# One load behind a transpose, one pair of norms ahead of a statistic: an order of work by hand in an MLP mixer kernel

## The chip, the cores and the metric

The kernel runs on one core of a Trainium2 chip. The core has five engines with instruction streams of their own: TensorE (PE; its weight loads are shown as PEld), VectorE (DVE), ScalarE (ACT), GpSimd (POOL) and SyncE (SP), which here only issues DMAs. They meet at semaphores. The metric is the device time of one execution in microseconds, as the median of several runs.

## The reference

The input x has 2048 tokens of 512 numbers in bf16; w1 and w2 are 512 by 512, w3 is 512 by 1792, w4 is 1792 by 512.

```
h  = gelu(layernorm(x) @ w1)
g0, g1, g2, g3 = the four quarters of h's 512 columns, shifted along
                 the tokens by +1, -1, +2, -2, zeros at the edge
x1 = x + concat(g0, g1, g2, g3) @ w2
out = x1 + gelu(layernorm(x1) @ w3) @ w4
```

The layer norms subtract the mean and divide by the square root of the variance plus 1e-5; they have no weights.

## The kernel before

The 2048 tokens are 16 tiles of 128. Tile t holds tokens t, t + 16, t + 32 and so on, one per partition, so that a shift by one or two tokens reads a neighbouring tile, and only the edges wrap. All weights and all tiles stay in SBUF. The eight PSUM banks are handed out by hand.

The first layer (norm, w1, gelu) is made in two ways.

Tiles 0 to 5 go raw: x is transposed as it is (tiles 0 to 3 by TensorE and ACT, `tp0` to `tp3` and `ev0` to `ev3`; tiles 4 and 5 by one transposing DMA straight from DRAM, `tdx_4`), multiplied by w1 (`m1r`, L378), copied to SBUF (`rc`, L388) and normed afterwards: `zr` (L393, DVE) takes off mean times column sum of w1, `g1r` (L399, ACT) scales and applies gelu, and a transposing DMA `th` (L357) puts the result in place. Their statistics are needed late.

Tiles 6 to 15 go in pairs and are normed first. For each tile DVE makes statistics `st0_t` (L289, bn_stats), and from them an aggregate `ag0_t` (L294); for each pair GpSimd raises the variances to the power of minus one half, `rs0_t` (L300); DVE applies both, `nm0_t` (L309). Pairs 8 and 10 are transposed by TensorE (`tp8`, `tp10`, L323) and evacuated by ACT (`ev8`, `ev10`, L332); pairs 6, 12 and 14 by a transposing DMA issued on SP, `td0_t` (L343). Then come a matmul with w1 per pair (`m1p`, L410) and gelu into a transposed buffer (`g1p` L420, or `g1s` L425 tile by tile).

The second product is `m2_t`, four matmuls per tile, one per shifted quarter; for tiles 8 to 15 it is cut into parts (L450), each of which waits for its own neighbours, and for tiles 0 to 7 not (L436). Tiles 14 and 15 need tiles 0 and 1 in their last parts, by the wrap of the tokens, and so wait for `th_0`. `x1_t` (L460, DVE) adds x. The second norm works as the first, with `td1` transposes. Tiles 8 to 15 come first in the second layer, then 0 to 7: `m3h_0_0_0` (L492), the first product with w3, takes tiles 8 and 9 and waits for `td1_8`. Then follow the products with w3 by blocks of four tiles (L468) and with w4 (L511), the last sum (L523) and the stores (L527).

The order on each engine is written out by hand: `firsts` (L637 to L652) names the operations of each engine in order, and what is not named follows as it was added. Nothing reorders them later; an engine that waits holds up all that stands behind it. Semaphore waits are derived from what each operation reads and writes. Nearly all DMAs are issued on SP, in the order of `firsts["sp"]`; the first loads of w1 and that of x1 on ACT's queue. A load `ldxT` may take several tiles (`load_x(t, n)`, L271): its consumers wait for the whole of it.

Around the change, SP issues the loads of x10, x11 and x12, then `td0_6`, which waits for `nm0_7`, then x13, x14 with x15, the four loads of w2, one for each 128 rows, then `td0_12` and `td0_14`. DVE meanwhile goes through statistics, aggregates and norms of tiles 6 to 15. On PE the six `m1r` are followed by `tp8`, `m1p6`, `tp10`, `m1p8`, `m1p10`.

Of the kernel before, what the change touches and what calls it, by code (L numbers as in the profile page):

```python
# [5 lines left out]
P = 128  # L6
# [20 lines left out]
class Program:  # L27
# [7 lines left out]
    def add(self, eng, name, fn, reads=(), writes=(), dma=False):  # L35
        self.ops.append(Op(name, eng, fn, reads, writes, dma))
# [135 lines left out]
def bass_standalone__mixer_s_mlp__prompt_kernel(nc: bass.Bass, x, w1, w2, w3, w4, out):  # L172
# [4 lines left out]
    DC = D // P  # L177
# [10 lines left out]
    with ExitStack() as es:  # L188
# [14 lines left out]
        w2_sb = sb("w2_sb", [P, DC, D], BF16)  # L203
# [41 lines left out]
        add = pr.add  # L245
# [25 lines left out]
        def load_x(t, n, eng="sp"):  # L271
            add(eng, f"ldx{t}", lambda e: e.dma_start(x_sb[:, t : t + n, :], xd[:, t : t + n, :]),  # L272
                writes=[(("x", i), 0) for i in range(t, t + n)], dma=True)
# [269 lines left out]
                writes=[(("w1", c), 0)], dma=True)  # L543

        def load_w2(c):
            add("sp", f"ldw2{c}", lambda e: e.dma_start(w2_sb[:, c, :], w2[P * c : P * (c + 1), :]),
                writes=[(("w2", c), 0)], dma=True)

        def load_w3a(c):
            add("sp", f"ldw3a{c}",  # L550
# [11 lines left out]
        load_w1(2, "act")  # L562
        load_w1(3, "sp")
        load_x(1, 1, "act")
        for t, n in ((6, 1), (7, 1), (2, 1), (8, 1), (3, 1), (9, 1), (10, 1), (11, 1), (12, 1), (13, 1), (14, 2), (4, 2)):
            load_x(t, n)
        for c in range(DC):
            load_w2(c)
        for c in range(DC):
            load_w3a(c)  # L570
# [56 lines left out]
        for t in (8, 10):  # L627
# [9 lines left out]
        firsts = {}  # L637
# [2 lines left out]
            m2_12b m2_13b m2_14a m2_15a m2_12 m2_13 m2_14b m2_15b m2_14 m2_15""".split()  # L640
        firsts["act"] = """ldw10 ldw12 ldx1 table ev0 ev1 rc0 ev2 ev3 rc1 rc2 rc3 rc4 rc5 ev8 cse g1p6 ev10 g1p8 g1s10 g1s11
            g1r0 g1r1 g1p12 g1p14 g2h_0_0_0 g2h_0_0_4 g1r2 g1r3 g2h_0_0_8 g2h_0_0_12 g1r4 g1r5""".split()
        firsts["dve"] = """pada padb padc padd pade padf st0_0 st0_6 st0_7 ag0_6 ag0_7
            st0_8 nm0_6 nm0_7 st0_9 ag0_8 ag0_9 st0_10 st0_11 nm0_8 nm0_9 ag0_10 ag0_11
            st0_12 nm0_10 nm0_11 st0_13 ag0_12 ag0_13 st0_14 st0_15 ag0_14 ag0_15 nm0_12 nm0_13 st0_1 ag0_0 ag0_1
            nm0_14 nm0_15 zr0 zr1 x1_8 x1_9 st1_8 st1_9 ag1_8 ag1_9 st0_2 nm1_8 nm1_9 st0_3 ag0_2 ag0_3 x1_10 x1_11 st1_10
            st1_11 ag1_10 ag1_11 x1_12 nm1_10 nm1_11 x1_13 x1_14 x1_15 zr2 zr3 st0_4 st0_5 ag0_4 ag0_5 zr4 zr5
            st1_12 st1_13 ag1_12 ag1_13""".split()
        firsts["pool"] = """ident0 ident1 neghalf stz ste rs0_6 rs0_8 rs0_10
            rs0_12 rs0_14 rs0_0 rs1_8 rs0_2 rs1_10""".split()  # L650
        firsts["sp"] = """ldx0 ldw11 ldx6 ldw13 ldx7 ldx2 ldx8 ldx3 ldx9 tdx_4 ldx10 ldx11 ldx12 td0_6 ldx13 ldx14 ldw20 ldw21 ldw22 ldw23 td0_12 td0_14 ldw3a0 ldw3a1
            ldw3a2 ldw3a3 th_0 td1_8 ldw3b ldx4 td1_10 th_2 th_4 td1_12 td1_14 ldw4""".split()  # L652

        slots = [4, 0, 2]
# [111 lines left out]
```

## Time and profile before

| what | us |
|---|---|
| median of 3 runs | 136.62 (136.54 to 136.63) |
| the profiled execution | 136.32 |
| its span, first to last instruction | 134.5 |
| PE busy | 130.8 |
| DVE busy | 58.3 |
| ACT busy | 46.8 |
| POOL busy | 12.5 |
| granted TensorE clock | 1.0 in the whole span |

Times within the profile are counted from the start of the span. A row of a timeline gives start, length, engine, line, operation, what is written and read, how many instructions in a row are merged, and in brackets the idle time of the engine before it and what ended it. SPq is the queue of SyncE: its rows are the time that it takes to issue a DMA, not the transfer. A DMA view gives the time from the issue to the landing of the last byte as the semaphore tells it. The chain of waits is followed back from the last instruction, at each step to what released it.

### The profile page before, as it was taken

How to read it: one execution, taken by the hardware profiler on the slowest of the kernel's cores; microseconds unless marked ns; L12 is line 12 of the kernel's file. 1: busy time of each engine (PE TensorE's matmuls, PEld its weight loads, DVE VectorE, ACT ScalarE, POOL GpSimd, SP SyncE). 2: the span in 40 equal slices, each digit the busy share in tenths (PEclk: the TensorE clock that was granted, in tenths of full speed). 3: DMA queues.
4: the chain of work that ended last, by engine and by line, in shares of the span. 5: the costliest groups of instructions: out<-in, count | busy, mean ns of one | idle time of the engine just before them, and what ended most of it. 6: DMA issues, size and time to landing. Idle time of an engine off the chain costs nothing.

```text
span 134.5 us, 1794 instructions
## 1 busy us (share of the span) xinstructions
PE 130.8 (97%) x719; PEld 69.6 (52%) x729; DVE 58.3 (43%) x135; ACT 46.8 (35%) x56; POOL 12.5 (9%) x25
## 2 busy tenths in 40 slices
PE   7999999999999999999999999999999999999993
PEld 2446857678884444444444444444444444444452
DVE  0689999799967777762222000122200002322222
ACT  3488871507962036550001555200066630000000
POOL 2042422220330012220000000000000000000000
PEclk9999999999999999999999999999999999999999
DMA  4999379984465984444121000011110001111121
GB/s 123 317 247 217 115 145 246 255 292 83 78 128 100 295 262 78 78 80 78 39 68 49 5 0 0 0 39 39 41 37 5 0 0 39 39 39 39 44 75 42
DMA packets 24376, 12.96 MB, mean 96 GB/s; under 512 B 16688, under 2 KB 23600, under 8 KB 24368
## 3 DMA queue, kind: packets, MB, share of 16 engines
q1 hardware_dynamic: 23792, 12.42, 36.5%
q10 hardware_dynamic: 576, 0.43, 1.0%
q8 instruction: 6, 0.10, 0.3%
q14 instruction: 2, 0.02, 0.1%
HBM read 6.82 MB, written 2.10 MB: 66 GB/s over the span
## 4 chain that ended last, share of the span: by engine, by line
PE 89%; SPq 4%; DMA 2%; DVE 2%; issue 1%
PE ps L511 36%; PE ps L468 27%; PE ps L492 9%; PE ps L410 7%; PE ps L436 5%; PE ps L450 5%; DMA x_sb<-in_x_dram 2%; SPq L272 2%; SPq L351 1%; DVE st L289 1%; PE ps L323 1%; SPq L542 1%; DVE xn L309 0%; DVE o_sb L523 0%
## 5 line engine op out<-in xcount | busy, mean ns | idle before, releaser
L511 PE MATMUL ps<-w_sb,h2T 128*128 128x512 bf16 (+2 forms) x232 | 48.1, 366 | 0.3
L523 DVE TENSOR_TENSOR o_sb<-ps,x_sb 128x512 bf16<-128x512 f32 (+2 forms) x17 | 11.2, 660 | 61.2 <-PE ps L511 61.2
L479 ACT ACTIVATE h2T<-ps 128x1024 bf16<-128x1024 f32 x21 | 21.5, 1023 | 46.2 <-PE ps L468 46.2
L468 PE MATMUL ps<-x1nT,w_sb 128*128 128x512 bf16 x168 | 36.7, 379 | 0.0
L511 PEld LDWEIGHTS ps<-w_sb,h2T 128*128 128x128 bf16 x238 | 22.8, 98 | 25.9
L468 PEld LDWEIGHTS ps<-x1nT,w_sb 128*128 128x128 bf16 x168 | 16.4, 98 | 19.8
L289 DVE BATCH_NORM_STATS2 st<-x_sb 128x6 f32<-128x512 bf16 x32 | 20.9, 682 | 4.1 <-DMA x_sb<-in_x_dram 4.0
L300 POOL TENSOR_TENSOR rstd<-mv,neghalf 128x2 f32<-128x2 f32 x16 | 11.6, 725 | 46.1 <-DVE mv L294 46.1
L492 PE MATMUL ps<-x1nT,w_sb 128*128 128x256 bf16 x112 | 12.4, 273 | 0.0
L492 PEld LDWEIGHTS ps<-x1nT,w_sb 128*128 128x128 bf16 x112 | 11.0, 98 | 1.5
L460 DVE TENSOR_TENSOR x_sb<-ps,x_sb 128x512 bf16<-128x512 f32 x16 | 10.6, 685 | 2.5 <-PE ps L436 1.5
L410 PE MATMUL ps<-xnT,w_sb 128*128 128x256 bf16 x80 | 9.2, 273 | 0.0
L503 ACT ACTIVATE h2T<-ps 128x1024 bf16<-128x1024 f32 (+1 forms) x8 | 7.1, 913 | 6.0 <-PE ps L492 6.0
L410 PEld LDWEIGHTS ps<-xnT,w_sb 128*128 128x128 bf16 x80 | 7.6, 98 | 1.2
L309 DVE TENSOR_SCALAR x1n<-x_sb,mv,rstd 128x512 bf16<-128x512 bf16 x16 | 5.9, 409 | 5.3 <-POOL rstd L300 5.3
L450 PE MATMUL ps<-w_sb,hTf 128*128 128x512 bf16 x30 | 7.0, 379 | 0.1
L436 PE MATMUL ps<-w_sb,hTf 128*128 128x512 bf16 x31 | 6.9, 379 | 0.1
L378 PE MATMUL ps<-w_sb,xnT 128*128 128x512 bf16 x23 | 6.0, 382 | 0.1
L420 ACT ACTIVATE hTf<-ps 128x1024 bf16<-128x1024 f32 x4 | 4.1, 1023 | 4.2 <-PE ps L410 4.2
L332 ACT ACTIVATE xnT<-ps 128x512 bf16<-128x512 bf16 (+1 forms) x6 | 4.4, 738 | 2.3 <-PE ps L323 2.2
L436 PEld LDWEIGHTS ps<-w_sb,hTf 128*128 128x128 bf16 x32 | 3.1, 98 | 3.6
L294 DVE BATCH_NORM_AGGREGATE mv<-st 128x2 f32<-128x9 f32 x32 | 5.0, 185 | 0.0
(28 smaller groups left out, 36.8 us busy)
## 6 DMA issues: line engine op xcount, KB each, us to landing
out_dram<-o_sb SPq DMA_DIRECT2D x15, 128.0 KB, 1.8
w_sb<-in_w_dram SPq DMA_DIRECT2D x1, 1792.0 KB, 7.7
x_sb<-in_x_dram SPq DMA_DIRECT2D x11, 128.0 KB, 3.3
w_sb<-in_w_dram SPq DMA_DIRECT2D x4, 256.0 KB, 4.2
w_sb<-in_w_dram SPq DMA_DIRECT2D x6, 128.0 KB, 3.5
w_sb<-in_w_dram SPq DMA_DIRECT2D x1, 768.0 KB, 4.8
x_sb<-in_x_dram SPq DMA_DIRECT2D x2, 256.0 KB, 4.4
w_sb<-in_w_dram ACTq DMA_DIRECT2D x2, 128.0 KB, 3.2
```

The costliest lines, as they stand in the source:

```text
L289: add("dve", f"st{layer}_{t}", lambda e: e.bn_stats(st9[:, i, 0:6], src[:, t, :]), reads=[(r, 0)], writes=[(("st6", i), 0)])
L300: lambda e: e.tensor_tensor(rstd[:, i : i + n], mv[:, i : i + n, 1], neghalf[:, 0:n], ALU.pow),
L410: ins = e.matmul(dst, w1_sb[:, c, P * fc : P * (fc + 1)], xnT[:, t : t + 2, c, :], start=(c == 0), stop=(c == DC - 1))
L436: ins = e.matmul(bank(b), hTf[:, c0 : c0 + P], w2_sb[:, j, :], start=(j == 0), stop=(j == DC - 1))
L450: ins = e.matmul(bank(b), hTf[:, w[0] : w[0] + P], w2_sb[:, j, :], start=first and n == 0, stop=last and n == len(js) - 1)
L460: lambda e: e.tensor_tensor(x1_sb[:, t, :], bank(b), x_sb[:, t, :], ALU.add),
L468: ins = e.matmul(bank(b), w3_sb[:, c, P * fc : P * (fc + 1)], x1nT[:, 4 * q : 4 * q + 4, c, :], start=(c == 0), stop=(c == DC - 1))
L479: lambda e: e.activation(h2T[:, fc : fc + 2, q % 2, :], src, ACT_F.Gelu_apprx_tanh),
L492: ins = e.matmul(dst, w3_sb[:, c, P * (fc + i) : P * (fc + i + 1)], x1nT[:, t : t + 2, c, :], start=(c == 0), stop=(c == DC - 1))
L503: lambda e: e.activation(h2T[:, fc : fc + n, q % 2, 256 * k : 256 * (k + 1)], src, ACT_F.Gelu_apprx_tanh),
L511: ins = e.matmul(ps[:, 512 * b : 512 * b + c1 - c0], h2T[:, fc, q % 2, P * i : P * (i + 1)], w4_sb[:, fc, c0:c1], start=(fc == 0), stop=(f ...
L523: lambda e: e.tensor_tensor(o_sb[:, k % 4, c0:c1], ps[:, 512 * b : 512 * b + c1 - c0], x1_sb[:, t, c0:c1], ALU.add),
```

## The change

Four edits to the order and to the loads, none to what is computed.

- DVE's order: `nm0_8` and `nm0_9` stand between `st0_10` and `st0_11` instead of after both. `ag0_6` stands before `st0_7` instead of after it. `st0_1` takes the place of `st0_12`, and `st0_12` stands with `st0_13` behind `nm0_11`.
- SP's order: the load of x12 stands behind `td0_6` instead of before it.
- x12 and x13 are one load of 256 KB instead of two of 128 KB.
- w2 comes in two loads of 256 KB instead of four of 128 KB. A part of `m2` then waits for the half in which its rows lie.

```diff
         def load_w2(c):
-            add("sp", f"ldw2{c}", lambda e: e.dma_start(w2_sb[:, c, :], w2[P * c : P * (c + 1), :]),
-                writes=[(("w2", c), 0)], dma=True)
+            add("sp", f"ldw2{c}",
+                lambda e: e.dma_start(w2_sb[:, c : c + 2, :],
+                                      w2[P * c : P * (c + 2), :].rearrange("(c p) f -> p c f", p=P)),
+                writes=[(("w2", c + i), 0) for i in range(2)], dma=True)
...
-        for t, n in ((6, 1), (7, 1), (2, 1), (8, 1), (3, 1), (9, 1), (10, 1), (11, 1), (12, 1), (13, 1), (14, 2), (4, 2)):
+        for t, n in ((6, 1), (7, 1), (2, 1), (8, 1), (3, 1), (9, 1), (10, 1), (11, 1), (12, 2), (14, 2), (4, 2)):
             load_x(t, n)
-        for c in range(DC):
+        for c in range(0, DC, 2):
             load_w2(c)
...
-        firsts["dve"] = """pada padb padc padd pade padf st0_0 st0_6 st0_7 ag0_6 ag0_7
-            st0_8 nm0_6 nm0_7 st0_9 ag0_8 ag0_9 st0_10 st0_11 nm0_8 nm0_9 ag0_10 ag0_11
-            st0_12 nm0_10 nm0_11 st0_13 ag0_12 ag0_13 st0_14 st0_15 ag0_14 ag0_15 nm0_12 nm0_13 st0_1 ag0_0 ag0_1
+        firsts["dve"] = """pada padb padc padd pade padf st0_0 st0_6 ag0_6 st0_7 ag0_7
+            st0_8 nm0_6 nm0_7 st0_9 ag0_8 ag0_9 st0_10 nm0_8 nm0_9 st0_11 ag0_10 ag0_11
+            st0_1 nm0_10 nm0_11 st0_12 st0_13 ag0_12 ag0_13 st0_14 st0_15 ag0_14 ag0_15 nm0_12 nm0_13 ag0_0 ag0_1
...
-        firsts["sp"] = """ldx0 ldw11 ldx6 ldw13 ldx7 ldx2 ldx8 ldx3 ldx9 tdx_4 ldx10 ldx11 ldx12 td0_6 ldx13 ldx14 ldw20 ldw21 ldw22 ldw23 td0_12 td0_14 ldw3a0 ldw3a1
+        firsts["sp"] = """ldx0 ldw11 ldx6 ldw13 ldx7 ldx2 ldx8 ldx3 ldx9 tdx_4 ldx10 ldx11 td0_6 ldx12 ldx14 ldw20 ldw22 td0_12 td0_14 ldw3a0 ldw3a1
```

## The prediction

> **What bounds the kernel now.** I read the page first, then the chain of waits, then the timeline of each engine around the one place where the chain leaves TensorE. The page's first part:
>
> ```profile
> PE 130.8 (97%) x719; PEld 69.6 (52%) x729; DVE 58.3 (43%) x135; ACT 46.8 (35%) x56; POOL 12.5 (9%) x25
> ```
>
> TensorE is busy nearly always, so an edit can only gain where PE has a hole, or lose by opening one. The chain that ended last, in order of time (start, length, what):
>
> ```profile
> 6.42 3.24 DMA x_sb<-in_x_dram
> ...
> 9.68 1.29 DVE st L289 x2
> 10.97 0.64 DVE xn L309 x2
> ...
> 11.66 0.62 PE ps L323 x8
> 12.28 1.81 PE ps L410 x16
> ```
>
> Before 11.66 us it runs over the load of x10, the statistics of tiles 10 and 11 and the two norms of pair 8; after 11.66 it is all PE to 132.2. The PE timeline there:
>
> ```profile
> 11.16 0.38 PE L378 MATMUL ps<-w_sb,xnT 128*128 128x512 bf16 x1
> 11.66 0.62 PE L323 MATMUL ps<-ident,xn 128*128 128x128 bf16 x8
> 12.16 1.92 PE L410 MATMUL ps<-xnT,w_sb 128*128 128x256 bf16 x16
> ```
>
> The durations include pipelining, so holes are read from starts. Matmuls of this 512-wide form start 0.216 us apart when nothing holds them (the 12 of tiles 3 to 5 start at 8.79, 9.01, 9.22 ...). The last of tile 5 started at 11.165; the next slot was 11.381, but the first transpose of pair 8 (tp8) started at 11.660. That hole is 0.279 us. The eight transposes start 0.056 apart, so the slot after them was 12.117; m1p6 started at 12.165, a hole of 0.048. Together 0.327. Behind that, PE starts follow without a hole to 28.27, and later ones are 0.05 at a time, tied to other PE work. So the most that these edits can win is about 0.33 us.
>
> What ended the two holes: VectorE and the queue of SyncE (SP).
>
> ```profile
> 5.89 0.69 DVE L289 BATCH_NORM_STATS2 st<-x_sb 128x6 f32<-128x512 bf16 x1 [0.23 <-DMA x_sb<-in_x_dram]
> 6.50 0.32 DVE L294 BATCH_NORM_AGGREGATE mv<-st 128x2 f32<-128x9 f32 x2
> ...
> 9.68 1.29 DVE L289 BATCH_NORM_STATS2 st<-x_sb 128x6 f32<-128x512 bf16 x2 [0.47 <-DMA x_sb<-in_x_dram]
> 10.88 0.72 DVE L309 TENSOR_SCALAR xn<-x_sb,mv,rstd 128x512 bf16<-128x512 bf16 x2
> ...
> 12.58 0.74 DVE L309 TENSOR_SCALAR xn<-x_sb,mv,rstd 128x512 bf16<-128x512 bf16 x2 [0.23 <-POOL rstd L300]
> ```
> ```profile
> 6.42 1.52 SPq L272 DMA_DIRECT2D x_sb<-in_x_dram  x3
> 8.41 1.24 SPq L343 DMA_TRANSPOSE xnT<-xn  x1
> 9.69 1.06 SPq L272 DMA_DIRECT2D x_sb<-in_x_dram  x2
> ...
> 16.43 2.68 SPq L343 DMA_TRANSPOSE xnT<-xn  x2
> 19.15 2.01 SPq L551 DMA_DIRECT2D w_sb<-in_w_dram  x4
> 21.20 1.61 SPq L357 DMA_TRANSPOSE hTf<-hraw  x1
> 23.65 1.32 SPq L343 DMA_TRANSPOSE x1nT<-x1n  x1
> ```
>
> nm0_9 ends at 11.602 and releases tp8. Pair 6's transpose td0_6, issued at 8.41, releases m1p6; the DMA view of that issue alone, and of the 256 KB load of x14 (issued 10.31):
>
> ```profile
> xnT<-xn SPq DMA_TRANSPOSE x1, 3.7
> ```
> ```profile
> x_sb<-in_x_dram SPq DMA_DIRECT2D x1, 256.0 KB, 3.9
> ```
>
> So td0_6 landed at 12.12, and m1p6 started 0.046 later: tp8 alone being earlier would gain nothing, since m1p6 would wait for td0_6 instead.
>
> **The change part by part.** The sum is made on the profiled execution (136.32 us: span 134.5 and 1.8 around it); the median of the runs is 136.62, 0.30 above, and I carry the difference over to it.
>
> *Pair 8's norms ahead of st0_11.* rs0_8 is done at 9.99, so nm0_8 follows st0_10 directly: DVE starts are 0.61 apart after a statistic and 0.31 after a norm, hence nm0_8 10.29, nm0_9 10.60 to 11.01, instead of 11.60. tp8 then waits for nothing but PE: 11.381, and m1p6's slot comes at 11.828. st0_11 moves to 10.92, ag0_11 ends near 11.84 instead of 11.77, rs0_10 and nm0_11 are 0.07 later (13.39); tp10 needs that at 13.58, so this costs nothing; if that cover of 0.19 were gone, it would cost its 0.07.
>
> *x12 behind td0_6.* td0_6's issue stays at 8.41 (it waits for nm0_7), but 128 KB no longer stand before it in the queue. Bounds for its landing: 12.12 if x12 was no hindrance; 8.41 + 3.2 = 11.6 by td0_12 and td0_14, which had no loads ahead and took 3.2. Between them: the four 128 KB loads of w2 landed 0.35 apart, so 128 KB less is 11.77. Either of the last two lets m1p6 have its slot (it needs 11.78). I take those: in the trace x12 landed at 10.96, 0.95 after x11, and td0_6's packets ran slowly in just that time (by the packets' sizes 58 and 46 GB/s in the two quarters of a microsecond from 10.25, against about 210 in td0_12). m1p6 then starts 11.828 instead of 12.165: −0.337 (the 0.327 and 0.010 of start latency). [...]
>
> *What follows on ACT* keeps up: ev8 starts at 12.08 (rc5 ends 12.18, overlapping 0.1) and ends 13.10; ev10, now behind a g1p6 from 13.785, ends 15.72; m1p10's slot is 15.78 and its release 15.73 + 0.046. All shift by 0.337.
>
> *One aggregate early.* ag0_6 at 5.69 instead of 6.505: but ag0_7 started at 6.624 on st0_7's end (6.600), and still does. Worth 0: ag0_6 lay in the latency of st0_7. Uncovered, it would be 0.12, the step between two aggregates.
>
> *st0_1 in the place of st0_12, x12-13 as one load.* Both statistics now stand behind nm0_11, at 13.30. The load is issued at 9.69, where x13 was. Bounds for its landing: 12.50 (x13's +2.8, 128 KB) and 14.5 (+4.8, the load of x4, also 256 KB, behind 768 KB of w3); nearest is x14's +3.9, so 13.63. DVE then waits W = 0.35 us (W from 0 to 1.2). Even at W = 0, td0_12 comes behind one statistic more: 16.91 instead of 16.43, and as a transpose holds SP 1.24 us, td0_14 issues at 18.19 + W instead of 17.88. Everything behind it on SP moves by 0.31 + W: the w3 loads, th_0 (landed 26.20; m2_14 now needs it at 27.29), td1_8. td1_8 landed at 27.12 and now at 27.43 + W; m3h_0_0 wants it at 28.273 − 0.337 = 27.94. td0_12 itself lands at 20.14 + W, m1p12's slot is 20.99. So up to W = 0.46 the price is 0; at my 0.35 the cover is 0.11. [...] By the row of x13, a split x12 would land at 12.50 and W would be 0; x14's row gives 0.35; the sum is −0.337 by either, and only the cover differs (0.46 or 0.11).
>
> *w2 as two loads.* Issued at about 10.8 and 11.3; two issues of about 0.43 go, with SP idle until 16.4 anyway. With 128 KB more ahead of them, last landing 15.65 + 0.35 at most 16.1; m2_8a needs it at 17.54. Worth 0, cover 1.4.
>
> Sum: −0.337 + 0 + 0 = 136.28 on the median (135.98 on the profiled time).
>
> **Rivals.**
> *A, td0_6 is not earlier.* For it: its queue still has x10 and x11 ahead, and other transposes that follow loads were slow (th_0 took 5.0). Against: x11 landed at 10.01 and its packets were over before td0_6 could send any (about 1.2 us after issue). At 12.12 the change gains 0: 136.62; in between, proportionally.
> *B, the wait for x12-13 eats the gain.* W between 0.46 and 1.07: m3h_0_0 waits for td1_8 on 27.43 + W, and the result is W − 0.46 − 0.337, so 136.28 to 136.89. For it: 0.11 of cover only. Against: x13 had landed in 2.8, and td0_6 ahead of this load ends sooner.
> *C, slower.* The same place, decided by W above 1.07, which is a landing after 14.37. With x4's +4.8, W = 1.2 and the time is 136.62 + 0.40 = 137.02; m1p12 then waits too, 0.40 at 20.99, which is part of it. For it: 256 KB loads here landed at +3.9, 4.1 to 4.5 and 4.8. Against: those of over 4.1 had 256 KB or more just ahead of them.
>
> **How the numbers follow.** 0.2% is 0.27 us, about what a measurement of this kernel can tell from no change. The forecast gives faster by 0.25%, little over it: any loss of 0.07 makes it "same". Chances: forecast 0.55 (136.22 to 136.35, its own range: 0.05 of measurement each way), A whole or in part 0.17, B 0.13, both within 0.2% for nearly all of their spread, C or another loss 0.15. Faster 0.55, same 0.30, slower 0.15. The range reaches from 136.15 (the cap of 0.34 and run to run differences, the profiled run being 0.30 under the median) to 136.90, the end of B, and leaves out C.
>
> **What the profile after would show.** Right: tp8 (L323 x8) near 11.38 with no hole before it, m1p6 (L410) near 11.83, td0_6 landing +3.2 to +3.4, all PE starts from there to 28.3 earlier by 0.33. Right on the side: aggregates of pair 6 no earlier; td0_12 issued near 17.3, td0_14 near 18.5. Wrong by A: m1p6 released by td0_6 at 11.9 or later. Wrong by B or C: DVE idle behind nm0_11 on the x load for over 0.5 us, and a hole on PE before L492 or before L410 at 21.

## The result and the profile after

The changed kernel took 136.92 us (median of 9 runs, 136.55 to 137.08), the kernel before beside it 136.56 (136.22 to 136.80): a ratio of 1.0026, 95% interval 1.0016 to 1.0037. It is slower, where 0.25% faster was forecast. In all that follows the medians are of all runs, while a ratio leaves out three runs in a slower state (one of the changed kernel with x12 and x13 apart, two of the changed kernel again) and is not the quotient of the two medians. The profiled execution took 136.55 us, its span 134.8, which is the fastest of the nine, so it is not a typical one. A second profile of the same kernel, taken in the experiments, took 137.20 (span 135.4). Both are read here.

The first part of the page, and the timeline of TensorE at pair 8, in the first profile of the changed kernel:

```profile
PE 131.1 (97%) x719; PEld 69.7 (52%) x729; DVE 58.5 (43%) x135; ACT 46.8 (35%) x56; POOL 12.6 (9%) x25
```
```profile
11.29 0.81 PE L378 MATMUL ps<-w_sb,xnT 128*128 128x512 bf16 x2
11.94 0.61 PE L323 MATMUL ps<-ident,xn 128*128 128x128 bf16 x8
12.38 1.80 PE L410 MATMUL ps<-xnT,w_sb 128*128 128x256 bf16 x15
```

The two holes are gone, as foreseen: the last L378 starts at 11.72, tp8 0.216 later, m1p6 in the slot after its eighth transpose. But tp8 starts at 11.94, later than in the kernel before (11.66), because the raw tiles in front of it ended 0.56 us later in this execution (by 11.94, where the next matmul's slot is, instead of 11.38). So the closed holes show as no gain here.

DVE and SP in the same profile, then DVE in the second profile:

```profile
12.70 0.73 DVE L309 TENSOR_SCALAR xn<-x_sb,mv,rstd 128x512 bf16<-128x512 bf16 x2 [0.24 <-POOL rstd L300]
14.14 1.29 DVE L289 BATCH_NORM_STATS2 st<-x_sb 128x6 f32<-128x512 bf16 x2 [0.71 <-DMA x_sb<-in_x_dram]
```
```profile
8.71 1.24 SPq L343 DMA_TRANSPOSE xnT<-xn  x1
9.99 1.06 SPq L272 DMA_DIRECT2D x_sb<-in_x_dram  x2
11.10 0.95 SPq L547 DMA_DIRECT2D w_sb<-in_w_dram  x2
17.69 2.62 SPq L343 DMA_TRANSPOSE xnT<-xn  x2
20.35 2.04 SPq L553 DMA_DIRECT2D w_sb<-in_w_dram  x4
22.44 1.24 SPq L357 DMA_TRANSPOSE hTf<-hraw  x1
24.16 1.81 SPq L343 DMA_TRANSPOSE x1nT<-x1n  x1
```
```profile
14.31 1.29 DVE L289 BATCH_NORM_STATS2 st<-x_sb 128x6 f32<-128x512 bf16 x2 [0.52 <-DMA x_sb<-in_x_dram]
```

DVE idles 0.71 and 0.52 us behind nm0_11 until x12-13 has landed (14.12 and 14.29). td0_12 is issued at 17.69 instead of 16.43, and everything that follows on SP is about 1.2 us later, up to th_0 (issued at 22.44 instead of 21.20). What that costs is in the second profile. Its timeline of TensorE, and its chain of waits at the same place:

```profile
18.18 3.40 PE L450 MATMUL ps<-w_sb,hTf 128*128 128x512 bf16 x15
22.18 3.67 PE L410 MATMUL ps<-xnT,w_sb 128*128 128x256 bf16 x32 [0.60 <-DMA xnT<-xn]
```
```profile
9.88 0.43 SPq L343
10.31 0.04 issue
10.35 3.94 DMA x_sb<-in_x_dram
14.29 0.02 issue
14.31 1.29 DVE st L289 x2
...
17.86 4.28 DMA xnT<-xn
22.14 0.05 issue
22.18 3.67 PE ps L410 x32
```

td0_12, issued at 17.86, landed 4.28 us later, and m1p12 waited for it: 0.76 us from slot (21.42) to start (the bracket shows less, since it counts from the modelled end of the matmul before). Here the chain leaves PE in the middle of the kernel, where in the profile before it was all PE. Followed back, it runs from td0_12 over the statistics of tiles 12 to 15 and the load of x12-13 to the issue of td0_6, behind which that load now stands.

A number that leaves the start of an execution out is the time from tp8 (first L323 x8) to the first L492. Without a hole it is 16.54 to 16.56 us; from the first L492 to the end of the span it is 106.2 to 106.3 in every profile but one. It stands in the table of the experiments as "tp8 to L492".

### The profile page after: what moved, and what is told of

It is laid out like the page before. It is cut to its first block, busy times and chain, and to the rows that moved or that the text cites. A ratio compares the mean times of both kernels' runs of the same rounds, so it can differ in the third digit from the quotient of the medians.

```text
span 134.8 us, 1789 instructions
## 1 busy us (share of the span) xinstructions
PE 131.1 (97%) x719; PEld 69.7 (52%) x729; DVE 58.5 (43%) x135; ACT 46.8 (35%) x56; POOL 12.6 (9%) x25
## 4 chain that ended last, share of the span: by engine, by line
PE 97%; issue 0%; DVE 0%
PE ps L511 36%; PE ps L468 27%; PE ps L492 9%; PE ps L410 6%; PE ps L436 5%; PE ps L450 5%; PE ps L378 4%; PE ps L534 2%; PE ps L323 2%; PE ps L366 1%; DVE o_sb L523 0%
## 5 line engine op out<-in xcount | busy, mean ns | idle before, releaser
L492 PE MATMUL ps<-x1nT,w_sb 128*128 128x256 bf16 x112 | 12.4, 273 | 0.0
L492 PEld LDWEIGHTS ps<-x1nT,w_sb 128*128 128x128 bf16 x112 | 11.0, 98 | 1.5
L410 PE MATMUL ps<-xnT,w_sb 128*128 128x256 bf16 x80 | 9.2, 273 | 0.0
L410 PEld LDWEIGHTS ps<-xnT,w_sb 128*128 128x128 bf16 x80 | 7.6, 98 | 1.2
L378 PE MATMUL ps<-w_sb,xnT 128*128 128x512 bf16 x23 | 6.4, 400 | 0.1
```

Source lines behind the costliest of these rows:

```text
L378: ins = e.matmul(bank(b), xnT[:, t, c, :], w1_sb[:, c, :], start=(c == 0), stop=(c == DC - 1))
L410: ins = e.matmul(dst, w1_sb[:, c, P * fc : P * (fc + 1)], xnT[:, t : t + 2, c, :], start=(c == 0), stop=(c == DC - 1))
L492: ins = e.matmul(dst, w3_sb[:, c, P * (fc + i) : P * (fc + i + 1)], x1nT[:, t : t + 2, c, :], start=(c == 0), stop=(c == DC - 1))
```

## The experiments

Theory 1: pairs 12 and 14 come late on DVE, hence on SP, and PE then waits for td0_12 or for td1_8. Rival 2: the difference lies in the start of the executions. Rival 3: it lies in w2's two loads. All kernels compute the whole output. Each group of four ran on one chip, with its own runs of the kernel before. The diffs show only the changed part of a long line.

| kernel | median us | before beside it | ratio (95%) | tp8 to L492 |
|---|---|---|---|---|
| before, first profile | | | | 16.61 |
| changed, first profile | 136.92 | 136.56 | 1.0026 (1.0016 to 1.0037) | 16.54 |
| norms first alone | 136.47 | 136.45 | 1.0003 (0.9991 to 1.0015) | 16.54 |
| changed, x12 and x13 apart | 137.24 | 136.45 | 1.0028 (1.0002 to 1.0053) | 17.64 |
| changed, w2 in four | 136.94 | 136.45 | 1.0037 (1.0024 to 1.0049) | 17.03 |
| before, w2 in two | 136.69 | 136.45 | 1.0021 (1.0004 to 1.0039) | 16.60 |
| changed, w3 ahead | 137.24 | 136.47 | 1.0041 (1.0022 to 1.0059) | 17.62 |
| before, w3 ahead | 136.47 | 136.47 | 0.9999 (0.9988 to 1.0011) | 16.55 |
| before, st0_12 late | 136.58 | 136.47 | 1.0005 (0.9993 to 1.0017) | 16.56 |
| changed again | 137.17 | 136.47 | 1.0049 (1.0026 to 1.0071) | 17.32 |
| x12 by ACT | 136.48 | 136.59 | 0.9994 (0.9983 to 1.0006) | 16.54 |
| changed, x12 by ACT | 136.87 | 136.59 | 1.0025 (1.0004 to 1.0046) | 16.78 |
| changed, norms of 12 sooner | 137.43 | 136.59 | 1.0069 (1.0045 to 1.0094) | 16.65 |
| before, two statistics ahead | 137.15 | 136.59 | 1.0027 (1.0012 to 1.0041) | 16.87 |

**Norms first alone.** Only DVE's order up to tile 11 of the change is kept.

```diff
-        firsts["dve"] = """pada padb padc padd pade padf st0_0 st0_6 st0_7 ag0_6 ag0_7
-            st0_8 nm0_6 nm0_7 st0_9 ag0_8 ag0_9 st0_10 st0_11 nm0_8 nm0_9 ag0_10 ag0_11
+        firsts["dve"] = """pada padb padc padd pade padf st0_0 st0_6 ag0_6 st0_7 ag0_7
+            st0_8 nm0_6 nm0_7 st0_9 ag0_8 ag0_9 st0_10 nm0_8 nm0_9 st0_11 ag0_10 ag0_11
```

> Of the change only the order on DVE is kept: pair 8's norms ahead of tile 11's statistics, one aggregate early; loads and SP's order as before. Theory 1 (the loss is in the load of x12-13: it lands at 14.1, DVE idles 0.7 us, and pairs 12 and 14 and all behind them on SP come 0.8 to 1.3 us later): tp8 is about 0.28 us earlier, m1p6 waits for td0_6, which still stands behind x12, so the time is that of the kernel before within 0.1 us. Rival 2 (the loss is from the start, where the TensorE clock rose to full at 6.17 us instead of 5.19 and the first loads landed 0.29 later, and would be met by any kernel): no difference between kernels beyond that of a rerun. Rival 3 (the loss is in w2's two loads): as before, 136.5 to 136.6.

136.47 against 136.45: no change. There was no hole at m1p6, though: td0_6 landed at 12.31, before the slot at 12.64, since the raw tiles ended late here too (tp8 at 12.19). The order alone gained nothing here, and not for the reason expected.

**The changed kernel with x12 and x13 apart.**

```diff
-(12, 2), (14, 2), (4, 2)):
+(12, 1), (13, 1), (14, 2), (4, 2)):
...
-td0_6 ldx12 ldx14
+td0_6 ldx12 ldx13 ldx14
```

> The changed kernel with x12 and x13 as two loads of 128 KB, both behind td0_6; all else as changed. Theory 1: x12 lands at about 12.8 (+2.8, the row of x13 before), DVE idles less than 0.1 us behind nm0_11, td0_12 is issued at about 17.0 instead of 17.7, and the time is 0.3 to 0.6 us under that of the changed kernel, so 136.3 to 136.6. Rival 2 and rival 3: as the changed kernel, 136.9.

A miss: 137.24, with a wide spread (135.93 to 138.42). The DVE timeline:

```profile
13.49 1.28 DVE L289 BATCH_NORM_STATS2 st<-x_sb 128x6 f32<-128x512 bf16 x2
14.68 0.31 DVE L294 BATCH_NORM_AGGREGATE mv<-st 128x2 f32<-128x9 f32 x2
15.49 0.69 DVE L289 BATCH_NORM_STATS2 st<-x_sb 128x6 f32<-128x512 bf16 x1 [0.49 <-DMA x_sb<-in_x_dram]
```

x12 landed at 12.90, as expected, and the wait at st0_12 was gone. It came back at st0_14: x14 now stood third behind td0_6 and landed at 15.46. td0_12 was issued at 17.65, no sooner, and PE waited 0.77 us for it and 0.25 before L492. So the loss does not need the merge: with the loads apart, DVE's wait moved on to the load behind them. The lowest times, 135.93 and 135.97, are under any of the runs of the kernel before in that group (136.09). The profile suggests why: its raw tiles ended at 11.36, and tp8 started there without a hole. Its span of 135.26 less the two waits would be 134.2, and the two fastest executions have 134.1. By this estimate a single execution can have the gain; no profile of such a one was taken.

**The changed kernel with w2 in four.**

```diff
-        for c in range(0, DC, 2):
+        for c in range(DC):
...
-ldw20 ldw22 td0_12
+ldw20 ldw21 ldw22 ldw23 td0_12
```

> The changed kernel with w2 as four loads again; x12-13 stays one load. Theory 1: as the changed kernel, 136.8 to 137.0. Rival 3: 0.3 us under it, 136.6. Rival 2: as the changed kernel.

136.94: the loss is there without the merge of w2, against rival 3. The chain of waits:

```profile
24.42 4.38 DMA x1nT<-x1n
28.80 0.14 issue
28.94 1.14 PE ps L492 x9
```

td1_8 landed at 28.80, and L492 started 0.31 us after its slot; th_0 (landed 27.92) had cost 0.16 before. In this execution td0_12 was in time (21.14), and the wait was at the later place.

**The kernel before with w2 in two.**

```diff
-        for c in range(DC):
+        for c in range(0, DC, 2):
...
-ldw20 ldw21 ldw22 ldw23 td0_12
+ldw20 ldw22 td0_12
```

> The kernel before with only w2 as two loads. Theory 1 and rival 2: as the kernel before, 136.5 to 136.6. Rival 3: 136.9.

136.69, 0.21% over the kernel before, its interval just clear of 1: between the expectations. Its profile has td1_8 landing at 28.30 and a hole of 0.05 us before L492, and that execution took 136.51. Two of its eleven runs, 137.62 and 137.12, have 2.6 us outside the span instead of 1.8; by the mean spans, 134.77 against 134.62, the kernel is 0.15 us behind. What w2's two loads cost by themselves is not settled; since the loss stays without them, they are not needed for it.

**w3 ahead of td0_12, in the changed kernel and in the kernel before.**

```diff
-ldw20 ldw22 td0_12 td0_14 ldw3a0 ldw3a1
-            ldw3a2
+ldw20 ldw22 ldw3a0 ldw3a1 td0_12 td0_14
+            ldw3a2
```

> The changed kernel with two of the four 256 KB loads of w3 issued ahead of td0_12, while SP has nothing else to issue. Theory 1, as it now stands (SP's queue behind td0_12 is late by 0.8 to 1.3 us, and PE waits before the first L492 for td1_8, as the kernel with w2 in four showed with a hole of 0.31 us): th_0 and td1_8 land about 1 us earlier than in the changed kernel (before 26.6 and 27.5), no hole before L492, and the time is 0.3 to 0.5 us under the changed kernel, 136.4 to 136.6. Waits for td0_12 or td0_14 at 21 to 23 us may stay. Rival 2 (the start of the TensorE clock alone decides) : as the changed kernel, 136.9.

> The same move of two w3 loads in the kernel before. Theory 1: there th_0 and td1_8 land over 1 us before they are needed, so the time stays within 0.1 us of 136.5. A rival in which earlier w3 helps any kernel: 0.3 us faster.

The cure failed in the time, 137.24. Where it was aimed, th_0 landed at 25.98 (27.18 in the changed kernel) and td1_8 at 27.88, later than the 27.5 expected; no hole was left before L492, to which PE now came a microsecond later. But x14 landed late (16.12, against 15.15 in the second profile of the changed kernel; the two loads of w3 had gone out at 12.51 and 13.01, close behind it). So td0_12 went out at 18.30, it took +4.09, and PE waited longer at the earlier place, 1.04 us:

```profile
11.03 5.09 DMA x_sb<-in_x_dram
...
18.30 4.09 DMA xnT<-xn
22.39 0.05 issue
22.44 3.67 PE ps L410 x32
```

The same move in the kernel before changed nothing (136.47 against 136.47), as expected: there td0_12 was issued at 17.15 and landed at 21.07, in time for m1p12 at 21.84.

**The kernel before with st0_12 late.**

```diff
-            st0_12 nm0_10 nm0_11 st0_13 ag0_12 ag0_13 st0_14 st0_15 ag0_14 ag0_15 nm0_12 nm0_13 st0_1 ag0_0 ag0_1
+            st0_1 nm0_10 nm0_11 st0_12 st0_13 ag0_12 ag0_13 st0_14 st0_15 ag0_14 ag0_15 nm0_12 nm0_13 ag0_0 ag0_1
```

> The kernel before with one edit on DVE: st0_1 and st0_12 change places, so that both statistics of pair 12 stand behind nm0_11; the loads stay, x12 has landed by 11. Theory 1: td0_12 is issued 0.5 us later, td0_14 and what follows on SP 0.3 later, without a wait of DVE for x12: from this alone 0 to 0.15 us slower, 136.5 to 136.65. If the order on DVE is the whole loss: 136.9.

136.58 against 136.47, interval across 1, as expected: this edit on DVE alone, which puts td0_12 at 16.95, is inside the cover. PE had no hole behind 12 us. This kernel and the second profile of the changed one started tp8 within 0.02 us of each other (11.84 and 11.82) and took 136.44 and 137.20: the 0.76 between them is the hole before L410. By rival 2 two executions with the same start should take the same time.

**The changed kernel again.** No edit.

> The changed kernel once more, for another execution's profile: DVE idles 0.5 to 1 us behind nm0_11 on the load of x12-13 and td1_8 lands at 28 or later. Theory 1: where the clock rises early and so the raw tiles end early, there is a hole on PE before L410 at 21 to 23 us or before L492; the time is 136.8 to 137.0. Rival 2: no hole, and a late clock.

137.17, ratio 1.0049, somewhat over the time expected. The hole is as theory 1 has it; the profile is shown above. td1_8 landed at 28.38, no longer late, since PE had already lost 0.76.

**x12 by ACT.** The norms of pair 8 first, x12 issued on ACT's queue between ev0 and ev1, all else as before.

```diff
         load_x(1, 1, "act")
+        load_x(12, 1, "act")
...
-ldw10 ldw12 ldx1 table ev0 ev1 rc0
+ldw10 ldw12 ldx1 table ev0 ldx12 ev1 rc0
...
-ldx10 ldx11 ldx12 td0_6
+ldx10 ldx11 td0_6
```

> The kernel before with pair 8's norms ahead of tile 11's statistics (and ag0_6 early) and the load of x12 issued by ACT between ev0 and ev1 instead of by SP ahead of td0_6; DVE's order of pairs 12 and 14, x13's load and w2 as before. Theory 1 (the two holes at tp8 and m1p6 are worth 0.33 us where the raw tiles end early, and the loss comes only from pairs 12 and 14 and SP's queue behind them): x12 lands before 10.5, td0_12 is issued within 0.3 us of the kernel before, td0_6 lands before 12.1, and the time is 0.1 to 0.3 us under the kernel before. If x12's packets now delay x10 and x11 by 0.3 or more: no gain.

136.48 against 136.59: the gain is not shown. x12 landed at 8.65, but x10 only at 10.32 (9.66 in the profile before), as the second half of the expectation has it, and td0_6 landed at 12.29. PE waited too, 0.33 us before tp3, for x3 (landed at 8.36, 7.52 in the profile before), and so the raw tiles ended only at 12.10. DVE stood waiting for x10:

```profile
10.34 0.70 DVE L289 BATCH_NORM_STATS2 st<-x_sb 128x6 f32<-128x512 bf16 x1 [0.42 <-DMA x_sb<-in_x_dram]
```

**The changed kernel with x12 by ACT.**

```diff
-(12, 2), (14, 2), (4, 2)):
+(13, 1), (14, 2), (4, 2)):
...
-td0_6 ldx12 ldx14
+td0_6 ldx13 ldx14
```

The load of x12 stands on ACT's queue as in the experiment before.

> The changed kernel with x12 loaded by ACT between ev0 and ev1, and x13 alone by SP behind td0_6; DVE's order and w2 as changed. Theory 1: DVE's wait behind nm0_11 falls from 0.5-0.7 us to under 0.2, td0_12 is issued near 17.1, and the time is 0.2 to 0.5 us under the changed kernel, 136.4 to 136.7. If the order on DVE is the cause: as the changed kernel, 136.9 to 137.1.

136.87, ratio 1.0025; inconclusive. DVE's wait for x12 was gone, but x10 at 10.50 made the norms of pair 10 0.4 to 0.8 us later than in the changed kernel's profiles, and td0_12 was issued at 17.69, as in the first of them. Lateness on SP stayed, from another cause: in this profile td0_12 landed in time (20.90), td1_8 at 28.74, and L492 waited 0.23 us. PE also waited 0.48 before tp3, for x3.

**The changed kernel with the norms of pair 12 sooner.**

```diff
-ag0_12 ag0_13 st0_14 st0_15 ag0_14 ag0_15 nm0_12 nm0_13 ag0_0 ag0_1
+ag0_12 ag0_13 st0_14 nm0_12 nm0_13 st0_15 ag0_14 ag0_15 ag0_0 ag0_1
```

> The changed kernel with nm0_12 and nm0_13 ahead of st0_15 and of pair 14's aggregates on DVE. td0_12 is issued 0.5 to 0.7 us sooner (near 17.2), td0_14 0 to 0.5 later. Theory 1 with td0_12 as the main wait of PE (holes of 0.76 and 0.77 us before L410 in two profiles): 0.2 to 0.4 us under the changed kernel, 136.5 to 136.8. If td1_8 is the main wait: as the changed kernel or slower, since td0_14 and all behind it are no sooner.

137.43 and no gain, as the second case had it. td0_12 went out at 16.86 and landed at 19.90, and no hole was left before L410. But td0_14 went out at 19.23, td1_8 landed at 28.50, and L492 waited 0.11. (The profiled execution, 138.13, has 1.5 us more at its end, where the last store took 2.95 us to land; in the first profile of the changed kernel it took 1.5. That is not part of this reading, and it leaves the size of this loss open.)

**The kernel before with two statistics ahead of nm0_12.** No load is touched.

```diff
-ag0_14 ag0_15 nm0_12 nm0_13 st0_1 ag0_0 ag0_1
+ag0_14 ag0_15 st0_1 st0_2 nm0_12 nm0_13 ag0_0 ag0_1
...
-ag1_8 ag1_9 st0_2 nm1_8
+ag1_8 ag1_9 nm1_8
```

> The kernel before with two statistics that are needed later, st0_1 and st0_2, put ahead of nm0_12 on DVE, and no load touched: td0_12 is issued 1.2 us later and td0_14 0.9 later, about as in the changed kernel. Theory 1: the loss of the changed kernel appears from this lateness alone: 136.8 to 137.2, with a hole on PE before L410 at 21 to 23 us or before L492. If the loads themselves (their size, or what they push aside in the DMA queue) are the cause: within 0.15 us of the kernel before.

137.15 against 136.59, ratio 1.0027: a loss like that of the changed kernel, from a later td0_12 and a later queue behind it, with the loads as they were. Its rows on SP and in the chain of waits:

```profile
17.95 2.61 SPq L343 DMA_TRANSPOSE xnT<-xn  x2
```
```profile
17.95 3.71 DMA xnT<-xn
21.66 0.04 issue
21.71 3.67 PE ps L410 x32
```

td0_12 issued at 17.95 landed at 21.66, and PE waited 0.31 us. With st0_12 late it was issued at 16.95 and cost nothing that could be measured; here, a microsecond later, there is a loss like the change's. The landing has a part in it: it took +3.71, and with the +3.2 of the profile before td0_12 would have been there at 21.15, ahead of the slot at 21.40.

## Why the prediction was wrong, point by point

Two terms of the sum failed: the gain was sized on one execution, and the price of the later transposes, put at nothing, was not nothing.

**The gain, −0.337.** The mechanism was right, the size was that of one execution. tp8 waits for no norm any more and m1p6 not for td0_6, as predicted. But the holes were as wide as 0.33 us only because the raw tiles ended at 11.38 in the profiled execution of the kernel before. Four later kernels have the order of the kernel before up to tp8 and the load of x12 ahead of td0_6 (w2 in two, w3 ahead of before, st0_12 late, two statistics ahead). Their raw tiles ended at 11.63 to 12.24, and their holes at tp8 were 0, 0, 0.04 and 0.16 us, at m1p6 none. TensorE in the second of these, w3 ahead of before, the last raw matmuls and tp8:

```profile
11.16 1.24 PE L378 MATMUL ps<-w_sb,xnT 128*128 128x512 bf16 x4
12.24 0.55 PE L323 MATMUL ps<-ident,xn 128*128 128x128 bf16 x7
```

The starts run on 0.216 apart, without a hole. So in these four executions the holes were worth 0 to 0.16, where I took the cap.

**td0_6 sooner without x12 before it.** Its landing was forecast as +3.2 to 3.4; it was +3.05 in both profiles of the changed kernel. But in those four kernels, with x12 ahead, it took +3.09 to +3.13 as well: td0_6 was issued at 9.03 to 9.42 there, behind nm0_7, instead of 8.41, and x12's packets had gone (it landed by 10.53). In norms first alone, with x12 ahead and td0_6 issued at 8.63, x12 landed at 10.96 as in the profile before, and td0_6 took +3.67; the changed kernel, in its first profile, issued it at 8.71 without x12 ahead, and it took +3.05. So the +3.7 goes with an early td0_6 close behind x12, and not with every execution. The difference is then 0.6 to 0.7, more than the 0.35 that I took. In norms first alone an earlier td0_6 would have gained nothing: m1p6 had its slot at 12.64, and td0_6 had landed at 12.31.

**ag0_6 early, 0.** Right: ag0_7 starts 0.034 after its own tile's statistic has ended, with ag0_6 long out of the way.

**w2 as two loads, 0.** The second half landed at 16.27 and 16.53 in the two profiles, past the bound of 16.1, and PE had no hole near 18, where m2_8a begins.

**W, the wait for x12-13.** Taken as 0.35, measured as 0.71 and 0.52 in the changed kernel. The load took +4.12 and +3.94, within the bounds of 2.8 to 4.8 and near the 3.9 that I chose. What I missed is its issue: 9.99 and 10.35 instead of 9.69. Behind td0_6 the load inherits the wait of td0_6 for nm0_7, and that one moves with the landing of x6 and x7 (x7's at 5.87 in the profile before, 5.94 to 6.88 in the others). Ahead of td0_6 x12 did not depend on it.

**The step that failed: the zero for "st0_1 in the place of st0_12, x12-13 as one load".** I wrote "up to W = 0.46 the price is 0; at my 0.35 the cover is 0.11". td0_12 came at 17.69 and 17.86, not 17.3; td0_14 at 18.97 and 19.15, not 18.5. And the covers had been counted with landings of +3.2, which td0_12 and td0_14 had in the profile before. Moved later, td0_14 took +4.03 and +3.91 and td0_12 +3.21 and +4.28. So in the second profile the wait appeared first before L410, which I had placed behind L492 in the order of covers (0.80 against 0.46). The late issue alone does not open that hole: at +3.2 td0_12 would have landed at 21.06, before the slot at 21.42. Among the fourteen profiles, six issued td0_12 by 17.0, and it took +3.05 to +3.29. Seven issued it at 17.65 or later; in three of them it took +3.20 or +3.21, in four +3.71 to +4.28, and just these four have the hole before L410, of 0.31 to 1.04 us. The fourteenth, w3 ahead of before, issued it at 17.15; it took +3.92 and was still in time. So the price that I put at 0 was that of a later issue into a time in which the transposes often landed later. The place named by rivals B and C, td1_8 before L492, is that of the kernel with w2 in four, and td0_12 before L410 stood in C as its second part. C's deciding point, a landing of the load after 14.37, was not needed: 14.12 and 14.29 were enough, because the issue of the load, the landing of the transposes and the order on DVE each added their part.

**The chances.** Slower had 0.15. The forecast asked that every cover on the path through SP hold, with 0.11 us on the last of them.

Not settled: the share of w2's two loads, how the mean loss divides between L410 and L492, and why the later transposes landed late. No kernel here beats the kernel before by more than its interval.

## What to carry to other kernels

A hole that one profile shows between two engines may belong to that execution (here 0.28 us before tp8 in one profile, 0 to 0.16 in four others with the same order up to there): read it in a second one before it is taken as the gain, and above all where the start decides which of the two is late, as it did here (the raw tiles ended between 11.36 and 12.24 in the fourteen profiles). A load that is moved behind a waiting DMA on the same queue can take over that wait, as x12-13 did (issued at 9.99 and 10.35, where x13 had been at 9.69), and pass it to everything that its consumer feeds (td0_12 issued at 17.69 and 17.86 instead of 16.43). Add up lateness along the whole queue, transposes and later loads included, and compare it with the cover at each place where the bound engine comes back to that queue. A cover counted with the landing time of one moment is too wide if the transfer, issued later, takes longer to land: here +3.23 for td0_12 in the profile before, and +3.71 to +4.28 in four of the seven profiles that issued it at 17.65 or later.

## What the runs showed of the hardware

- **The start.** The same instructions on PE ran at half rate (512-wide starts 0.427 us apart instead of 0.216) until quite different times: the trace's clock record turned to full at 5.19 in the profile before, at 6.17 and 3.41 in the two of the changed kernel, and between 3.40 and 6.79 in the others that have the record. The granted clock of 1.0 in the whole span, as the page and the table of the kernel before have it, leaves this start out: in the profile before, the first entry of the clock record is the one at 5.19. What sets that time was not shown. An early clock did not always bring an early end of the raw tiles: of the five profiles with full rate by 3.6, one ended them at 11.36, the others at 11.63 to 11.84, against 11.38 in the profile before with 5.19. In the second profile of the changed kernel PE, at full rate by 3.41, waited for x1 before tp1 and started tp8 at 11.82 all the same.

```profile
4.67 0.60 PE L378 MATMUL ps<-w_sb,xnT 128*128 128x512 bf16 x2
5.96 0.40 PE L323 MATMUL ps<-ident,x_sb 128*128 128x128 bf16 x4 [0.68 <-DMA x_sb<-in_x_dram]
```

- **Late transposes.** The page's DMA part lists a few packets of the kind "instruction":

```profile
q14 instruction: 2, 0.02, 0.1%
```

One of the two, 8 KB, starts between 19.7 and 21.8 us in every profile of this case. In the profile before it came at 21.67, when td0_14 had landed (21.05, +3.17). In the first of the changed kernel it came at 21.33, among the last packets of td0_14, which then took +4.03; in the second at 20.96, and td0_12 took +4.28; with x12 and x13 apart at 20.22, and td0_12 took +4.11; with two statistics ahead at 19.73, and td0_12 took +3.71. In the last three there followed, 0.6 to 1.2 us after it, quarters of a microsecond in which only 8 to 11 packets of the transposes started, against some 200 before. That is a coincidence in time, which was not tried by an experiment, and it is not the only one. td0_6 in the profile before had slow quarters too (57 and 45 packets, from 10.25) with no such packet near. td0_12 of w3 ahead of before (+3.92) was slow at 19.4 to 19.9, before that packet; there another of the kind, 16 KB on q8, had come at 18.20 with td0_12's first packets, and a load of w3 landed at 18.70.
